# Two PSUM tiles for the transposes of batch 1, and the kv step of batch 2 after matmul 14 instead of 12

## Chip, cores and metric

The kernel runs on one core of a Trainium2 chip. Its time is the device time of one execution in microseconds, and lower is better. Before the change the median of three runs is 281.68 us (281.46 to 281.71).

## What is computed

The inputs q, k and v have the shape (batch 8, heads 8, sequence 576, head size 64). Per batch and head, q is put through a softmax over the head size, k through a softmax over the sequence; k's softmax and v make a 64×64 matrix kv, and q's softmax is multiplied by it. The result, with the heads side by side, is a matrix x of 4608 tokens by 512, which goes through two dense layers with an exact Gelu between them.

```python
q_s = exp(q - max(q, -1));  q_s = q_s / (sum(q_s, -1) + 1e-9)
k_s = exp(k - max(k, 2));   k_s = k_s / (sum(k_s, 2) + 1e-9)
kv  = einsum('bhsd,bhse->bhde', k_s, v)
x   = einsum('bhsd,bhde->bhse', q_s, kv)       # -> (4608, 512)
out = gelu(x @ w_in) @ w_out                   # 512 -> 2048 -> 512
```

## The kernel before

**Tiling.** Each batch is a block of 512 tokens; the 64 tokens left over of each of the 8 batches make a ninth block. For every block TensorE does an h phase (`h_phase`, line 300: 16 groups of four 128×512 matmuls with w_in, each group followed by a Gelu on ScalarE, line 305) and a y phase (`y_phase`, line 310: four output tiles `j`, each the sum of 16 matmuls with w_out, counted by `t`, then a copy by VectorE at line 317 and a store).

**The attention part of a batch b** is cut into small steps that are placed between those matmuls:
- `exp_q`, `exp_k` (lines 133, 138): exponentials on ScalarE, into `eq` and `ek`.
- `norm_q` (lines 196 to 198): row sums, reciprocals and the product, on VectorE and POOL; with two parts the second product is on VectorE.
- `cast_v` (line 145): v to bf16 with a column of ones, into `v_aug`, one call for each of the four head pairs.
- `kv_step`: `kv_mm` twice (line 166, 36 small matmuls each, half 0 for head pairs 0 and 1, half 1 for 2 and 3), then `kv_norm` on VectorE (lines 176, 177), which writes `kvc`.
- The transpose of q. Batches 0 and 1 do it on TensorE, in two halves of eight 128×128 transposes (`tp_mm`, line 217), each copied out of PSUM by `tp_evac` (line 226 on VectorE). Later batches use a transposing DMA (`xbar_step`, line 236).
- `x_all`, or for batch 1 single calls of `x_mm` (line 256): kv times transposed q, copied out at lines 280 and 282.

**Buffers in PSUM.** Three pools: `psum_h` with three buffers of tag "h", `psum_y` with two of tag "y", and `psum_a`, which has one buffer for each of its tags: "a", and the larger "a2". A tile of `psum_a` can be written only when the last reader of the tile before it under the same tag is done. Under "a2" come, in turn: kv of batch 0, the transposes `tp` of batch 1, kv of batch 1, two tiles of x of batch 1, kv of batch 2 and so on. Under "a" come one half of batch 0's transposes, then a tile of x of each batch.

**Order.** The order on each engine is the program's own order (`manual_schedule`): an engine works through its instructions as they are written down and waits on semaphores where another engine's result, or the release of a buffer, is needed. The transposes of batch 1 are placed in the y phase of batch 0, after twelve of the sixteen matmuls of all four output tiles:

```python
for t in range(12):
    y_part(t, range(J))
tp_step(1, 0)             # tp_mm, tp_evac of half 0
tp_step(1, 1)
cast_v(1, 3)
load(3)
cast_wo(3, wo[3], 2, 1, "s")
y_part(12, range(J))
y_part(13, range(J))
kv_step(1)
```

`cast_wo(..., "s")` (line 412) is the conversion of a quarter of the last 512 rows of w_out on ScalarE. In the y phase of batch 1, steps hang on the pair (j, t): they are issued after that matmul. The exponentials of batches 2 and 3 stand before this phase in the order exp_q(2), exp_k(2), exp_k(3), exp_q(3).

Of the kernel before, what the change touches and what calls it, by code (L numbers as in the profile page):

```python
# [9 lines left out]
BF16 = mybir.dt.bfloat16  # L10
# [6 lines left out]
def kernel(  # L17
# [20 lines left out]
    J = 4  # L38
# [16 lines left out]
    psum_a = ctx.enter_context(tc.tile_pool(name="psum_a", bufs=1, space=bass.MemoryType.PSUM))  # L55
# [25 lines left out]
    st = [dict() for _ in range(B + 1)]  # L81
# [72 lines left out]
    def kv_mm(b, half):  # L154


        if "kv" not in st[b]:
            st[b]["kv"] = psum_a.tile([128, 2, 2, 256], FP32, tag="a2", name="kv")
        ps = st[b]["kv"]
        for n in range(NS):  # L160
            for i in range(2):
                for hh in range(2):
                    hp = 2 * half + i
                    pr = slice(hh * 64, hh * 64 + 64)
                    c = slice((hh ^ i) * 64, (hh ^ i) * 64 + 64)
                    nc.tensor.matmul(  # L166
                        ps[c, i, half, 0:D + 1], ek[b % 2][pr, hp, n, :],
                        v_aug[b % 2][pr, hp, n, 0:D + 1], start=(n == 0), stop=(n == NS - 1),
                    )

    def kv_norm(b, h0, h1):

        ps = st[b]["kv"]
        m = h1 - h0
        rec = small.tile([128, 2, 2], FP32, tag="reck")
        nc.vector.reciprocal(rec[:, :, 0:m], ps[:, :, h0:h1, D])
        nc.vector.tensor_tensor(  # L177
            out=kvc[b].rearrange("p (h i) d -> p i h d", i=2)[:, :, h0:h1],
            in0=ps[:, :, h0:h1, 0:D],
            in1=rec[:, :, 0:m].unsqueeze(3).to_broadcast([128, 2, m, D]), op=ALU.mult,  # L180
        )

    def kv_step(b):
        kv_mm(b, 0)
        kv_mm(b, 1)
        kv_norm(b, 0, 2)

    def norm_q(b, i=0, n=1, eng=None):

        eng = eng or nc.gpsimd  # L190
        eq = st[b]["eq"]
        w = H // n
        hs = slice(i * w, (i + 1) * w)
        qsum = small.tile([128, J, w], FP32, tag="qsum")
        recq = small.tile([128, J, w], FP32, tag="recq")
        nc.vector.reduce_sum(out=qsum, in_=eq[:, :, hs, :], axis=AX.X)  # L196
        nc.vector.reciprocal(recq, qsum)  # L197
        eng.tensor_tensor(  # L198
            out=eq[:, :, hs, :], in0=eq[:, :, hs, :],
            in1=recq.unsqueeze(3).to_broadcast([128, J, w, D]), op=ALU.mult,  # L200
        )

    def tp_mm(b, half):
        if half == 0:
            st[b]["qT"] = attn_sb.tile([128, J, HP, 128], BF16, tag="qT", name="qT")
        if b == 1:
            if half == 0:
                st[b]["tp"] = psum_a.tile([128, 2, J, 2, 128], BF16, tag="a2", name="tp")
            ps = st[b]["tp"][:, half]
        else:  # L210
            pool, tag = (psum_h, "h") if half == 1 else (psum_a, "a")
            ps = pool.tile([128, J, 2, 128], BF16, tag=tag)
        st[b][f"tp{half}"] = ps
        for i in range(2):
            hp = 2 * half + i
            for j in range(J):
                nc.tensor.transpose(
                    ps[:, j, i, :],
                    st[b]["eq"][:, j, 2 * hp:2 * hp + 2, :].rearrange("p h d -> p (h d)"),
                    identity,  # L220
                )
# [8 lines left out]
    def tp_step(b, half):  # L230
        tp_mm(b, half)
        tp_evac(b, half)

    def xbar_step(b):
        st[b]["qT"] = attn_sb.tile([128, J, HP, 128], BF16, tag="qT", name="qT")
        nc.sync.dma_start_transpose(
            out=st[b]["qT"].rearrange("p j x m -> p (j x) m"),
            in_=st[b]["eq"].rearrange("p j h d -> p (j h d)"),
        )
# [218 lines left out]
    norm_q(0, 0, 2)  # L458
    norm_q(0, 1, 2, nc.vector)
    tp_mm(0, 0)  # L460
    tp_evac(0, 0, "s")
    table(AF.Gelu)
# [4 lines left out]
    cast_wi(0, wi[0], "p")  # L467
    cast_wi(1, wi[1], "p")
    tp_mm(0, 1)
    warm(2)  # L470
    for hp, pool, tag in ((0, psum_y, "y"), (1, psum_y, "y"), (2, psum_a, "a"), (3, psum_h, "h")):
# [38 lines left out]
    for t in range(12):  # L510
# [35 lines left out]
    y_phase(1, {  # L546
        (0, 15): [lambda: norm_q(2, 0, 2)],
        (1, 1): [lambda: norm_q(2, 1, 2, nc.vector)],
        (1, 12): [lambda: kv_step(2)],
        (1, 15): [lambda: xbar_step(2)],  # L550
        (2, 2): [lambda: cast_v_all(3), lambda: load(4)],
        (3, 5): [lambda: x_all(2), lambda: kv_step(3)],
# [65 lines left out]
```

The softmax here doesn't subtract the row's maximum and nothing guards it: scores larger than these inputs give would overflow.

## Time and profile before

| | |
|---|---|
| median of three runs | 281.68 us (281.46 to 281.71) |
| profiled execution | 281.9 us |
| its span, first to last instruction | 280.1 us |
| TensorE clock granted | 1.00 |
| TensorE busy | 271.0 us, 97% of the span |
| ScalarE busy | 157.0 us, 56% |
| VectorE busy | 102.2 us, 37% |
| POOL busy | 33.0 us, 12% |
| h matmuls (line 300) | 576, busy 126.4 us |
| y matmuls (line 310) | 560, busy 124.2 us |

Matmuls overlap in the profile: one of 128×512 shows 379 ns, while the next starts about 216 ns after it. What a step takes of TensorE's time is therefore read from start to start. The names of engines in the profile are PE (TensorE matmuls), PEld (TensorE weight loads), DVE (VectorE), ACT (ScalarE), POOL and SP; `a <- b` in brackets names what ended an idle time. Times in a timeline are counted from the first instruction of the span.

### The profile page before, as it was taken

How to read it: one execution, taken by the hardware profiler on the slowest of the kernel's cores; microseconds unless marked ns; L12 is line 12 of the kernel's file. 1: busy time of each engine (PE TensorE's matmuls, PEld its weight loads, DVE VectorE, ACT ScalarE, POOL GpSimd, SP SyncE). 2: the span in 40 equal slices, each digit the busy share in tenths (PEclk: the TensorE clock that was granted, in tenths of full speed). 3: DMA queues.
4: the chain of work that ended last, by engine and by line, in shares of the span. 5: the costliest groups of instructions: out<-in, count | busy, mean ns of one | idle time of the engine just before them, and what ended most of it. 6: DMA issues, size and time to landing. Idle time of an engine off the chain costs nothing.

```text
span 280.1 us, 4564 instructions
## 1 busy us (share of the span) xinstructions
PE 271.0 (97%) x1922; PEld 125.2 (45%) x1922; DVE 102.2 (37%) x152; ACT 157.0 (56%) x243; POOL 33.0 (12%) x25
## 2 busy tenths in 40 slices
PE   7699989999999999999999999999999999999995
PEld 3344444444544444444444444444444444444443
DVE  3767477308763530074007500552005200230012
ACT  5747664779466915692469436852683264036400
POOL 1530050002020040005000500050005000000000
PEclk9999999999999999999999999999999999999999
DMA  6999999961997129911991189126501500120033
GB/s 235 380 404 427 400 401 407 399 250 43 268 390 91 41 76 240 357 41 42 259 372 41 42 209 375 53 77 171 131 0 75 150 2 0 75 77 0 0 77 76
DMA packets 44996, 50.10 MB, mean 179 GB/s; under 512 B 20400, under 2 KB 29872, under 8 KB 44720
## 3 DMA queue, kind: packets, MB, share of 16 engines
q1 hardware_dynamic: 44688, 49.68, 53.4%
q8 instruction: 15, 0.25, 0.4%
q10 hardware_dynamic: 288, 0.13, 0.2%
q14 instruction: 5, 0.04, 0.1%
HBM read 36.70 MB, written 9.44 MB: 165 GB/s over the span
## 4 chain that ended last, share of the span: by engine, by line
PE 75%; DMA 18%; SPq 2%; ACT 2%; ACTq 0%; issue 0%; DVE 0%
PE ps L310 36%; PE ps L300 35%; DMA w<-in_moe_w_in_dram 6%; DMA f<-in_v_dram 4%; DMA w<-in_moe_w_out_dram 3%; DMA out_dram<-y_sb 3%; SPq L98 2%; DMA touch<-in_moe_w_out_dram 2%; PE kv L166 1%; PE ps L332 1%; PE ps L256 1%; ACT ek L138 1%; ACT e L133 1%; ACTq L435 0%; ACT L133 0%
## 5 line engine op out<-in xcount | busy, mean ns | idle before, releaser
L300 PE MATMUL ps<-xT,wi_bf 128*128 128x512 bf16 x576 | 126.4, 379 | 0.2
L310 PE MATMUL ps<-wo_bf,g 128*128 128x512 bf16 x560 | 124.2, 379 | 0.0
L305 ACT ACTIVATE g<-ps 128x512 bf16<-128x512 f32 x144 | 85.2, 597 | 69.3 <-PE ps L300 69.3
L300 PEld LDWEIGHTS <-wi_bf 128*128 128x128 bf16 x576 | 56.1, 98 | 69.0 <-DVE wi_bf L383 1.0
L310 PEld LDWEIGHTS <-g 128*128 128x128 bf16 x560 | 54.0, 98 | 64.6 <-issue 0.8
L317 DVE COPY y_sb<-ps 128x512 f32<-128x512 f32 x35 | 23.8, 686 | 80.9 <-PE ps L310 80.7
L198 POOL TENSOR_TENSOR e<-e,recq 128x2048 bf16<-128x2048 bf16 (+1 forms) x9 | 25.7, 2857 | 179.2 <-DVE recq L197 151.0
L145 DVE CAST v_aug<-f 128x576 bf16<-128x576 f32 x26 | 17.9, 745 | 46.4 <-DMA f<-in_v_dram 46.4
L196 DVE TENSOR_REDUCE qsum<-e 128x16 f32<-128x1024 bf16 (+1 forms) x13 | 21.0, 1614 | 15.0 <-ACT e L133 15.0
L282 ACT CAST xT<-ps 128x512 bf16<-128x512 f32 x19 | 10.2, 589 | 27.9 <-PE ps L256 18.2
L133 ACT ACTIVATE e<-f 128x512 bf16<-128x512 f32 (+1 forms) x42 | 20.5, 556 | 2.4 <-DMA f<-in_q_dram 2.1
L138 ACT ACTIVATE ek<-f 128x2304 bf16<-128x2304 f32 (+1 forms) x10 | 17.2, 1730 | 1.9 <-DMA f<-in_k_dram 1.9
L280 DVE CAST xT<-ps 128x512 bf16<-128x512 f32 x15 | 9.7, 686 | 17.7 <-PE ps L256 14.8
L79 ACT ACT_TABLE_LOAD x9 | 11.5, 1283 | 2.8 <-issue 2.6
L133 ACT ACT_TABLE_LOAD x7 | 9.0, 1283 | 0.1
L417 PE MATMUL ps<-zeros 128*128 128x512 f32 (+1 forms) x14 | 7.1, 647 | 1.5 <-DVE zeros L449 1.5
L383 DVE CAST wi_bf<-w 128x512 bf16<-128x512 f32 x12 | 7.4, 660 | 2.5 <-DMA w<-in_moe_w_in_dram 2.2
L166 PEld LDWEIGHTS <-ek 64*64 64x64 bf16 x576 | 6.3, 105 | 3.0 <-issue 1.4
L166 PE MATMUL kv<-v_aug,ek 64*64 64x65 bf16 x576 | 6.9, 193 | 0.3
L198 DVE TENSOR_TENSOR e<-e,recq 128x1024 bf16<-128x1024 bf16 x4 | 6.4, 1608 | 0.1
L256 PE MATMUL ps<-qT,kvc 64*64 64x512 bf16 x60 | 5.0, 390 | 1.0 <-DVE kvc L177 1.0
L410 DVE CAST wo_bf<-w 128x2048 bf16<-128x2048 f32 (+1 forms) x4 | 4.4, 1090 | 3.8 <-DMA w<-in_moe_w_out_dram 3.8
(35 smaller groups left out, 42.4 us busy)
## 6 DMA issues: line engine op xcount, KB each, us to landing
out_dram<-y_sb SPq DMA_DIRECT2D x32, 256.0 KB, 2.3
f<-in_k_dram SPq DMA_DIRECT2D x6, 1152.0 KB, 9.7
f<-in_v_dram SPq DMA_DIRECT2D x6, 1152.0 KB, 11.8
f<-in_q_dram SPq DMA_DIRECT2D x6, 1024.0 KB, 7.5
w<-in_moe_w_in_dram SPq DMA_DIRECT2D x6, 512.0 KB, 8.9
f<-in_k_dram SPq DMA_DIRECT2D x4, 576.0 KB, 10.1
f<-in_v_dram SPq DMA_DIRECT2D x8, 288.0 KB, 7.9
f<-in_q_dram SPq DMA_DIRECT2D x4, 512.0 KB, 12.5
```

Of the source, the lines that this page charges most:

```text
L79: nc.scalar.activation(out=scr[:, 1:2], in_=scr[:, 0:1], func=func)
L133: nc.scalar.activation(out=dst[:, i], in_=src[:, u], func=AF.Exp)
L138: nc.scalar.activation(out=ek[b % 2][:, i:i + n], in_=st[b]["kf"][:, i:i + n].rearrange("p x (n d) -> p x n d", n=NS), func=AF.Exp,)
L145: eng.tensor_copy(out=v_aug[b % 2][:, hp, :, 0:D], in_=st[b]["vf"][:, hp, :].rearrange("p (n d) -> p n d", n=NS),)
L166: nc.tensor.matmul(ps[c, i, half, 0:D + 1], ek[b % 2][pr, hp, n, :], v_aug[b % 2][pr, hp, n, 0:D + 1], start=(n == 0), stop=(n == NS - 1),)
L196: nc.vector.reduce_sum(out=qsum, in_=eq[:, :, hs, :], axis=AX.X)
L198: eng.tensor_tensor(out=eq[:, :, hs, :], in0=eq[:, :, hs, :], in1=recq.unsqueeze(3).to_broadcast([128, J, w, D]), op=ALU.mult,)
L282: nc.scalar.copy(out=st[b]["xT"][:, hp, :], in_=ps)
L300: nc.tensor.matmul(ps, wi_bf[:, dm, t * 128:(t + 1) * 128], xT[:, dm, :], start=(dm == 0), stop=(dm == NDM - 1),)
L305: nc.scalar.activation(out=g[:, t, :], in_=ps, func=AF.Gelu)
L310: nc.tensor.matmul(ps, st[c]["g"][:, t, j * 128:(j + 1) * 128], wo_bf[:, t, :], start=(t == 0), stop=(t == NDF - 1),)
L317: nc.vector.tensor_copy(out=y_sb, in_=ps)
```

## The change

Two edits. First, `tp_mm` no longer makes one "a2" tile for both halves of batch 1's transposes. Half 0 takes a tile of its own under tag "a", as half 0 of batch 0 does, and half 1 takes a tile under "a2" and uses its first part. Second, the `kv_step` of batch 2 is issued after the matmul (1, 14) of the y phase of batch 1 instead of after (1, 12).

```diff
     def tp_mm(b, half):
         if half == 0:
             st[b]["qT"] = attn_sb.tile([128, J, HP, 128], BF16, tag="qT", name="qT")
-        if b == 1:
-            if half == 0:
-                st[b]["tp"] = psum_a.tile([128, 2, J, 2, 128], BF16, tag="a2", name="tp")
-            ps = st[b]["tp"][:, half]
+        if b == 1 and half == 1:
+            ps = psum_a.tile([128, 2, J, 2, 128], BF16, tag="a2", name="tp")[:, 0]
         else:
             pool, tag = (psum_h, "h") if half == 1 else (psum_a, "a")
             ps = pool.tile([128, J, 2, 128], BF16, tag=tag)
@@
         (0, 15): [lambda: norm_q(2, 0, 2)],
         (1, 1): [lambda: norm_q(2, 1, 2, nc.vector)],
-        (1, 12): [lambda: kv_step(2)],
+        (1, 14): [lambda: kv_step(2)],
         (1, 15): [lambda: xbar_step(2)],
```

## The prediction

> **What bounds the kernel now.** I read the page's busy shares first, then the waits of TensorE, then the stretches around the two edits in order of time, engine by engine.
>
> ```profile
> PE 271.0 (97%) x1922; PEld 125.2 (45%) x1922; DVE 102.2 (37%) x152; ACT 157.0 (56%) x243; POOL 33.0 (12%) x25
> ```
>
> TensorE is busy 97% of 280.1 us and the next engine 56%. A microsecond taken off TensorE's queue therefore comes off the time, unless something else is late at the same place. So all waits of TensorE are listed:
>
> ```profile
> PE ps L217 <- POOL e L198: 2.0, 1, 2.0
> PE ps L417 <- DVE zeros L449: 1.5, 1, 1.5
> PE ps L256 <- DVE kvc L177: 1.0, 2, 0.6
> PE tp L217 <- DVE qT L226: 0.8, 1, 0.8
> ```
>
> The first three belong to the start-up. The fourth is the only one after it, and it carries the name of the tile that the change splits. In order of time, TensorE first, then VectorE:
>
> ```profile
> 39.65 0.61 PE L217 MATMUL tp<-identity,e 128*128 128x128 bf16 x8
> 41.05 0.61 PE L217 MATMUL tp<-identity,e 128*128 128x128 bf16 x8 [0.78 <-DVE qT L226]
> 41.49 1.89 PE L310 MATMUL ps<-wo_bf,g 128*128 128x512 bf16 x8
> 43.31 0.78 PE L166 MATMUL kv<-v_aug,ek 64*64 64x65 bf16 x72
> 44.02 1.25 PE L310 MATMUL ps<-wo_bf,g 128*128 128x512 bf16 x5
> ```
>
> ```profile
> 40.30 0.69 DVE L226 COPY qT<-tp 128x1024 bf16<-128x1024 bf16 x1 [0.66 <-PE tp L217]
> 41.69 0.69 DVE L226 COPY qT<-tp 128x1024 bf16<-128x1024 bf16 x1 [0.70 <-PE tp L217]
> 42.30 0.74 DVE L145 CAST v_aug<-f 128x576 bf16<-128x576 f32 x1
> ```
>
> The second eight transposes begin 0.05 us after the copy of the first eight ends at 40.99. Half 1 writes columns that the copy does not read, yet it waits for it.
>
> The second edit is at batch 2's kv. No TensorE wait is listed there, but the weight loads show one, and the chain says on whom:
>
> ```profile
> 66.92 0.67 PEld L166 LDWEIGHTS <-ek 64*64 64x64 bf16 x72 [0.62 <-ACT ek L138]
> ```
>
> ```profile
> 64.86 2.02 ACT ek L138
> 66.88 0.04 issue
> 66.92 0.78 PE kv L166 x67
> 67.70 5.50 PE ps L310 x25
> ```
>
> kv starts 0.04 us after the exponential of k(2) ends. The idle time of the weight loader overstates the stall, since it normally rests between loads; it is worked out below.
>
> **What the Trainium skill says.** *PSUM — Partial Sum Buffer*, "PSUM bank collisions raise a hardware error", forbids two engines on one bank and quadrant at once, and its "Specifications" give 2 KiB to a bank. Each half is 4·2·128 bf16 = 2,048 bytes, so the halves are in two banks before and after: the wait hangs on the shared tile, not on the bank. *TensorE: Matmul & The Clock Gate*, "Back-to-back issue gap", gives N/2.4 + 2.5 ns for isolated matmuls, 56 ns at 128 columns, and about 81 ns for streams that reload weights; here eight transposes start over 0.61 − 0.22 = 0.39 us, which is 56 ns each, so I use that. *TensorEngine Tiling (Array Packing)*, "Key Properties", says that a change of tiling mode drains TensorE; the trace agrees: eight L310 matmuls and the change to 64-row tiles take 43.31 − 41.49 = 1.82 us, where the chain's 45 matmuls in 9.71 us (0.216 each) give 1.73, so the change costs 0.09.
>
> **The change part by part.** *Half 1 in its own tile.* From the first transpose of a half to the matmul after it is 41.49 − 41.05 = 0.44 us. Half 0 starts at 39.65, so half 1 could start at 40.10 and starts at 41.05: **0.95 us** of TensorE's time goes. The trace does not show transposes following a different tile's without a wait. Bounds: 0.056 us between the two (as inside a half), or 0.31 us, the largest step at a change of shape seen above; there is none here, so I take the first, and 0.7 is the low end. A gain above 0.95 is excluded, as nothing else stands before half 1: its input is normalized by 39.03 (VectorE's 1.73 us multiply from 37.30).
>
> The buffers moved into are free: half 0 takes tag "a", last read in batch 0; half 1 takes "a2", last read by batch 0's kv. The readers that come next on them wait for copies that end before: batch 1's x on "a" comes after 44, and kv on "a2" needs only the copy of half 1.
>
> What is late next, with TensorE 0.95 earlier (kv at 42.36, its second half, where v's last quarter is first used, 0.32 later, at 42.68):
> - VectorE: the copy of half 0 stays at 40.30; half 1's follows back to back at 40.91 (at 45.31 two L317 copies of 0.68 take 1.29 together, so start 0.61 apart) and ends at 41.60; the cast of v's last quarter can then start at 41.52. Its transfer was issued at 33.1 and took 8.3, so it landed at 41.4 to 41.5: it fits within hundredths. The cast ends at 42.26, 0.4 before its use.
> - TensorE's queue: kv waits for half 1's copy (41.60), and the sequencer stood at that wait at 42.42 before, so would reach it at 41.47 and is held some 0.15 us. Three L310 matmuls lie issued ahead (0.65 us), so it costs nothing; without that cover, 0.15.
> - ScalarE's casts of the last two quarters of w_out: landings at 34.46 + 7.6 = 42.1 and 35.9 + 6.8 = 42.7, casts done at 42.74 and 43.37. Their matmuls, at 44.02 and 44.89, move to 43.07 and 43.94: 0.3 and 0.6 are left.
> - kv's normalization is done at 44.79; moved by 0.95 it stays ahead of x. From there to the kv of batch 2, no wait of TensorE is listed; the exponentials of batch 2 follow the last Gelu, which TensorE releases, so they move too. k(2) and q(2) land before 49.
>
> *kv of batch 2 two matmuls later.* By the spacing, 29 L310 matmuls from 60.38 and the 0.09 change put kv at 60.38 + 6.26 + 0.09 = 66.73; it started at 66.92: a stall of **0.19**. Two more matmuls are 0.43, so kv comes at 67.16 against a release at 66.92: the stall goes with 0.24 to spare. The step carries 72 matmuls (0.71 us), their loads, and on VectorE a reciprocal (0.17) and a product (0.42); no DMA. Between its old and new place only the two matmuls are issued, so the order on VectorE, ScalarE, POOL and SP is as before, and the q transpose by DMA still follows it. VectorE's reciprocal, which with everything behind it waits for kv, started at 68.39, behind the 1.22 us multiply from 67.25. kv's last matmul now starts 0.59 after its first, at 67.75, and 0.26 later (43.89 to 44.15 in batch 1) VectorE can act: 68.01. The multiply hides it, with 0.39 to spare. If that cover were gone, the y copy and four casts behind would shift by the 0.24, and the last cast (to 72.26) would still precede its use by kv of batch 3 at 73.59 − 0.19 by 0.9. The transposed q landed at 68.64 + 3.7 = 72.38; x needs it at 73.14 − 0.19: 0.56 left.
>
> Sum: 0.95 + 0.19 = 1.14 us. The profiled execution took 281.9 (span 280.1), 0.2 above the median of the runs; I take the gain off both: profile 280.76 with a span of 278.96, median 281.68 − 1.14 = **280.54**.
>
> **Rivals.** *Transfers take over* (0.10): v's last quarter or w_out's third lands later than in this trace. The four v transfers took 8.3 to 9.4 us, so a slip of 0.5 to 1 is conceivable; 0.4 and 0.3 are free. It costs 0.2 to 0.7: 280.7 to 281.2. Against it: the stream was issued before, at its own pace, and no engine of the change touches it. *The kv move gives nothing* (0.06): the exponential ends later against TensorE, or the stall is another; 281.68 − 0.95 = 280.73. *The wait is inherited* (0.05): half 1 is still ordered after half 0's copy, through the two-bank tag or otherwise; only 0.19 is left, 281.49, within what counts as no change. *Slower* (0.03): kv of batch 2 comes so late that its normalization holds VectorE, and with it the casts of v(3) that kv of batch 3 needs. That begins where kv is 0.24 + 0.39 + 1.14 = 1.8 us later than before (1.14 is from 72.26 to 73.40), and takes 1.14 more to cancel the gain; 4 us later would give 281.68 − 1.14 + 2.2 = 282.7. Two matmuls are a ninth of that. The forecast itself has 0.76.
>
> **How the numbers follow.** A measurement of this kernel tells about 0.2%, 0.56 us, from no change. Faster: 0.76 + 0.06 + 0.08 of the transfers' 0.10 = 0.90; within: 0.02 + 0.05 = 0.07; slower 0.03. The range runs from 280.30, below the forecast by the spread of the three runs (0.25), to 280.95, which takes in the low end of the first step (0.25 less), the rival without the kv gain, and half of the transfers'.
>
> **What would show it.** In the profile after: the wait of L217 on L226 is gone and sixteen transposes start within 0.9 us; VectorE's two L226 copies stand back to back; the cast of v starts near 41.5; kv of batch 1 starts near 42.36. Batch 2's kv follows 31 L310 matmuls, without an idle time put down to the exponential, 0.31 us after the last of them. From there on every start is 1.14 earlier. The forecast is wrong if kv of batch 1 shows a wait for v or L412 holds L310 after it, if a transpose waits on L226 or L177, or if x of batch 2 waits for the q transpose.

## The result, and the profile after

The changed kernel takes 280.44 us (280.29 to 280.69, six runs) against 281.69 (281.43 to 282.0, six runs): a ratio of 0.9956, 95% interval 0.9943 to 0.9969, a gain of 1.25 us. Measured again further below, it is 280.42 against 281.59. The forecast was 280.54 in 280.30 to 280.95. The profiled span went from 280.1 to 278.9 us.

The busy shares of the page after, and all waits of TensorE after (columns: who waited for whom, total us, times, longest). Its line numbers are smaller by two than those of before, for all that stands after the first edit: L215 are the transposes, L308 the y matmuls, L298 the h matmuls, L254 x.

```profile
PE 272.2 (98%) x1922; PEld 125.8 (45%) x1922; DVE 102.1 (37%) x152; ACT 157.0 (56%) x243; POOL 33.0 (12%) x25
```

```profile
PE ps L415 <- DVE zeros L447: 1.5, 1, 1.5
PE ps L254 <- DVE kvc L177: 1.0, 2, 0.6
PE ps L215 <- POOL e L198: 0.4, 1, 0.4
```

Only the waits of the start-up are left. The one of the transposes on the copy, 0.8 us before, is gone. It was a wait that the program carried: before, the first transpose of half 1 waits on VectorE's semaphore, and in the changed kernel it carries no wait for VectorE. The timeline at the transposes, TensorE and then VectorE (start, duration, what):

```profile
39.52 0.61 PE L215 MATMUL ps<-identity,e 128*128 128x128 bf16 x8
39.97 0.61 PE L215 MATMUL tp<-identity,e 128*128 128x128 bf16 x8
40.42 1.89 PE L308 MATMUL ps<-wo_bf,g 128*128 128x512 bf16 x8
42.24 0.78 PE L166 MATMUL kv<-v_aug,ek 64*64 64x65 bf16 x72
42.95 1.47 PE L308 MATMUL ps<-wo_bf,g 128*128 128x512 bf16 x6
```

```profile
40.17 0.69 DVE L224 COPY qT<-ps 128x1024 bf16<-128x1024 bf16 x1 [0.65 <-PE ps L215]
40.78 0.68 DVE L224 COPY qT<-tp 128x1024 bf16<-128x1024 bf16 x1
41.38 0.75 DVE L145 CAST v_aug<-f 128x576 bf16<-128x576 f32 x1
```

Half 1 follows half 0 after 0.45 us, where it was 41.05 − 39.65 = 1.40: 0.95 us. The copies stand back to back, 0.61 apart, and v's cast behind them. That cast is held by two things at once: v's last quarter, issued at 33.00, landed at 41.36, 0.02 before it. The casts of the last two quarters of w_out's last 512 rows, on ScalarE:

```profile
42.02 1.25 ACT L410 CAST wo_bf<-w 128x512 bf16<-128x512 f32 x2 [2.12 <-DMA w<-in_moe_w_out_dram]
```

The first of the two (0.62 us) ends at 42.64, and the y matmul that needs it, the one behind kv, starts at 42.95: 0.31 later. The timeline of TensorE at kv of batch 2, and the only wait of the weight loader there:

```profile
59.30 6.85 PE L308 MATMUL ps<-wo_bf,g 128*128 128x512 bf16 x31
66.09 0.78 PE L166 MATMUL kv<-v_aug,ek 64*64 64x65 bf16 x72
66.80 5.14 PE L308 MATMUL ps<-wo_bf,g 128*128 128x512 bf16 x23
71.86 0.63 PE L254 MATMUL ps<-qT,kvc 64*64 64x512 bf16 x8
```

```profile
PEld L166 <- ACT ek L138: 0.4, 1, 0.4
```

kv starts 66.09 − 59.30 = 6.79 us after the first of 31 matmuls, which at 0.216 each take 6.70: the 0.09 of the change of tiling mode and nothing else. The weight loader still shows a wait that is put down to the exponential, 0.4 where it was 0.6. That is not a stall: the loader rests 0.42 before x of batch 2 as well, where the profile names nobody. Only the 0.2 above that was lost time. The exponential itself ended at 65.80, 0.29 before kv; where kv waits for it, kv starts 0.05 after it ends.

The chain that ended last, over the stretch of both edits (start, us, what). Before, it left TensorE at kv of batch 2 for the exponential. Now TensorE hands over to itself from 22.89 on:

```profile
22.89 6.43 PE ps L298 x29
29.33 10.36 PE ps L308 x48
39.69 0.45 PE ps L215 x8
40.13 0.45 PE tp L215 x8
...
59.47 6.69 PE ps L308 x31
66.16 0.71 PE kv L166 x68
```

From the first transpose of batch 1 to x of batch 2 TensorE took 73.14 − 39.65 = 33.48 us before and 71.86 − 39.52 = 32.34 after: **1.14 us**, the sum of the prediction. Another 0.13 lies ahead of the transposes, in the start-up, which neither edit touches, and 0.06 is lost behind x (207.04 us from x to the end of the span instead of 206.98), which makes the 1.21 of the span.

### The profile page after: what moved, and what is told of

It reads as the page before. It is cut to its first block, busy times and chain, and to the rows that moved or that the text cites. A ratio compares the mean times of both kernels' runs of the same rounds, so it can differ in the third digit from the quotient of the medians.

```text
span 278.9 us, 4564 instructions
## 1 busy us (share of the span) xinstructions
PE 272.2 (98%) x1922; PEld 125.8 (45%) x1922; DVE 102.1 (37%) x152; ACT 157.0 (56%) x243; POOL 33.0 (12%) x25
## 4 chain that ended last, share of the span: by engine, by line
PE 91%; DMA 7%; DVE 1%; ACTq 0%; issue 0%
PE ps L308 44%; PE ps L298 42%; DMA w<-in_moe_w_in_dram 3%; DMA f<-in_v_dram 2%; PE kv L166 2%; DMA touch<-in_moe_w_in_dram 2%; PE ps L254 1%; PE ps L330 1%; DVE wi_bf L381 0%; ACTq L433 0%; PE ps L259 0%; PE ps L215 0%; PE tp L215 0%; DVE y_sb L335 0%; PE xx L254 0%
## 5 line engine op out<-in xcount | busy, mean ns | idle before, releaser
L298 PE MATMUL ps<-xT,wi_bf 128*128 128x512 bf16 x576 | 126.4, 379 | 0.3
L308 PE MATMUL ps<-wo_bf,g 128*128 128x512 bf16 x560 | 124.2, 379 | 0.0
L298 PEld LDWEIGHTS <-wi_bf 128*128 128x128 bf16 x576 | 56.2, 98 | 68.9 <-DVE wi_bf L381 1.0
L308 PEld LDWEIGHTS <-g 128*128 128x128 bf16 x560 | 53.9, 98 | 64.6 <-issue 0.8
L415 PE MATMUL ps<-zeros 128*128 128x512 f32 (+1 forms) x14 | 8.6, 764 | 1.5 <-DVE zeros L447 1.5
L254 PE MATMUL ps<-qT,kvc 64*64 64x512 bf16 x60 | 5.0, 390 | 1.0 <-DVE kvc L177 1.0
```

The costliest lines, as they stand in the source:

```text
L298: nc.tensor.matmul(ps, wi_bf[:, dm, t * 128:(t + 1) * 128], xT[:, dm, :], start=(dm == 0), stop=(dm == NDM - 1),)
L308: nc.tensor.matmul(ps, st[c]["g"][:, t, j * 128:(j + 1) * 128], wo_bf[:, t, :], start=(t == 0), stop=(t == NDF - 1),)
```

## The experiments

All are read in the same way. "Begin" is the start of the first transpose of batch 1; "half" is from there to that of half 1; "kv(2)" is from the matmul before kv of batch 2 to kv; "to x" is from the begin to x of batch 2. Ratios are to the kernel before, measured together with it (its median was 281.69 for the first row of the changed kernel, 281.57 for the four rows from "tiles only" to "shared tile, slow copy", 281.59 for the others). Several of these differences in time are inside each other's intervals; the steps of the traces tell them apart.

| kernel | begin | half | kv(2) | to x | median | ratio (95%) |
|---|---|---|---|---|---|---|
| before | 39.65 | 1.39 | 0.51 | 33.48 | | |
| changed | 39.52 | 0.45 | 0.31 | 32.34 | 280.44 | 0.9956 (0.9943 to 0.9969) |
| tiles only | 39.74 | 0.45 | 0.51 | 32.54 | 280.74 | 0.9969 (0.9958 to 0.9980) |
| kv only | 39.58 | 1.39 | 0.31 | 33.29 | 281.39 | 0.9993 (0.9983 to 1.0003) |
| shared tile, copies last | 39.07 | 0.45 | 0.51 | 32.66 | 280.60 | 0.9963 (0.9950 to 0.9976) |
| shared tile, slow copy | 39.05 | 1.71 | 0.51 | 33.80 | 281.83 | 1.0013 (1.0002 to 1.0024) |
| v's cast late | 39.45 | 0.45 | 0.31 | 33.16 | 281.18 | 0.9982 (0.9973 to 0.9991) |
| kv after (1, 10) | 39.56 | 0.45 | 0.94 | 32.97 | 281.00 | 0.9981 (0.9974 to 0.9988) |
| kv after (1, 13) | 38.97 | 0.45 | 0.31 | 32.47 | 280.39 | 0.9961 (0.9946 to 0.9976) |
| changed, again | 39.28 | 0.45 | 0.31 | 32.34 | 280.42 | 0.9955 (0.9940 to 0.9969) |
| v's quarter last | 40.19 | 0.45 | 0.31 | 33.23 | 281.42 | 0.9996 (0.9982 to 1.0011) |

**The tiles alone.** The diff against the changed kernel:

```diff
-        (1, 14): [lambda: kv_step(2)],
+        (1, 12): [lambda: kv_step(2)],
```

> The two tiles alone, kv of batch 2 where it was, after matmul (1, 12). Theory (two waits, which add): half 1's transposes follow half 0's 0.056 us apart, 0.95 us of TensorE's time goes, and kv of batch 2 still starts 0.04 us after the exponential of k(2), 0.51 us after the matmul before it. Time 281.69 - 0.95 = 280.74. Rival (the kv stall depends on where the transposes leave TensorE, so the first edit shortens it too): kv of batch 2 starts 0.31 us after the matmul before it, and the time is that of the changed kernel, 280.5. Rival (part of the gain of 1.25 is not of the edits): half 1 gains 0.95 or less and the time stays above 280.9.

From its timeline of TensorE:

```profile
39.74 0.61 PE L215 MATMUL ps<-identity,e 128*128 128x128 bf16 x8
40.19 0.61 PE L215 MATMUL tp<-identity,e 128*128 128x128 bf16 x8
59.52 6.42 PE L308 MATMUL ps<-wo_bf,g 128*128 128x512 bf16 x29
66.07 0.78 PE L166 MATMUL kv<-v_aug,ek 64*64 64x65 bf16 x72
```

It went as the theory has it: 33.48 − 32.54 = 0.94 us "to x", and kv of batch 2 keeps its step of 0.51. The time is 0.83 below that of before. The second wait does not shrink with the first, because the exponential moves with TensorE: in all eleven profiled executions it ends 6.50 us after the first y matmul of batch 1.

**kv alone.** The diff against the kernel before:

```diff
-        (1, 12): [lambda: kv_step(2)],
+        (1, 14): [lambda: kv_step(2)],
```

> kv of batch 2 after matmul (1, 14) alone, the transposes in their shared tile. Theory: kv starts 0.31 us after the matmul before it, where it was 0.51, and its first matmul 0.2 us after the exponential's end; half 1's transposes still wait 0.78 us for the copy of half 0. Gain 0.2 us: 281.5, hardly to be told from no change by the time; the starts in the trace decide. Rival: the stall moves with kv (it is not the exponential that it waits for), 0.51 us again, 281.7.

From its timeline of TensorE:

```profile
40.98 0.61 PE L217 MATMUL tp<-identity,e 128*128 128x128 bf16 x8 [0.78 <-DVE qT L226]
67.09 0.78 PE L166 MATMUL kv<-v_aug,ek 64*64 64x65 bf16 x72
```

The wait of the transposes is there, that of kv is not: 0.20 us "to x". By the time alone, 0.18 with an interval over 1, it could not have been told. The two edits add: 0.94 + 0.20 = 1.14.

**One tile, copies after both halves.** The diff against the kernel before:

```diff
-    tp_step(1, 0)
-    tp_step(1, 1)
+    tp_mm(1, 0)
+    tp_mm(1, 1)
+    tp_evac(1, 0)
+    tp_evac(1, 1)
```

> The kernel before, with its one tile for both halves, and both copies issued after both halves of transposes; kv of batch 2 stays at (1, 12). Theory (half 1 waits only because it stands after the copy of half 0 on the same tile): the sixteen transposes run without a wait, 0.95 us goes as with two tiles. If the copy of half 0 waits for all sixteen, the copies start at about 40.75 on VectorE instead of 40.30, the cast of v's last quarter ends 0.45 later, at 42.7, and kv's second half waits for it by less than 0.1. Time 280.7 to 280.85. Rival (half 1 waits for something else of the one tile, its buffer or its bank): a wait of TensorE in the transposes remains, 281.5 or more.

The timeline of TensorE, and of VectorE:

```profile
39.07 1.06 PE L217 MATMUL tp<-identity,e 128*128 128x128 bf16 x16
```

```profile
40.17 1.29 DVE L226 COPY qT<-tp 128x1024 bf16<-128x1024 bf16 x2 [0.92 <-PE tp L217]
41.37 0.74 DVE L145 CAST v_aug<-f 128x576 bf16<-128x576 f32 x1
```

With one tile and the same two banks the sixteen transposes run without a wait: what held half 1 was its place behind the copy on a shared tile. The first copy starts 40.17 − 39.07 = 1.10 us after the first transpose, where it is 0.65 with two tiles; so it waits for all sixteen. Two tiles let VectorE start on half 0 at once.

What that is worth the run does not show. kv takes 0.85 us to the next matmul instead of 0.71, so 0.14 is lost, but the wait that ends last there is another one. From the timelines of TensorE and ScalarE:

```profile
41.79 0.86 PE L166 MATMUL kv<-v_aug,ek 64*64 64x65 bf16 x72
42.63 1.46 PE L310 MATMUL ps<-wo_bf,g 128*128 128x512 bf16 x6
```

```profile
41.97 1.25 ACT L412 CAST wo_bf<-w 128x512 bf16<-128x512 f32 x2 [2.97 <-DMA w<-in_moe_w_out_dram]
```

kv's second half waits some 0.06 us for v's cast, as expected ("less than 0.1"). The y matmul behind kv needs the first of ScalarE's two casts of the last rows of w_out (their third quarter), which ends at 42.58, and it starts 0.05 after that. This execution began its transposes 0.45 earlier than the changed kernel's, but w_out's quarter came only 0.05 earlier (41.97 against 42.02). By these numbers two tiles would have lost as much here. The time, 280.60, is not told apart from the 280.74 of the tiles alone. One tile with the copies last and kv after (1, 14) was not run.

**One tile, a slower copy.** The diff against the kernel before:

```diff
-    tp_step(1, 0)
+    tp_mm(1, 0)
+    tp_evac(1, 0, "s")
```

> The kernel before, with half 0 copied by ScalarE instead of VectorE, which took 0.99 us for such a copy in batch 0 against 0.69; ScalarE is idle there from 39.99 to 42.12. Theory (the stall is the copy's length and two signals): half 1's transposes start 0.3 us later than before, 1.25 us of stall against 0.95, and the time rises by 0.3 to 282.0. VectorE has one copy less, so its cast of v is not later. Rival (the stall hangs on VectorE's queue or on a fixed cost of changing halves): half 1 starts as before or earlier, 281.7 or less.

TensorE's and ScalarE's timelines:

```profile
40.76 0.61 PE L217 MATMUL tp<-identity,e 128*128 128x128 bf16 x8 [1.10 <-ACT qT L228]
```

```profile
39.70 1.01 ACT L228 COPY qT<-tp 128x1024 bf16<-128x1024 bf16 x1 [0.54 <-PE tp L217]
```

The copy is 0.32 longer (1.01 against 0.69) and half 1 starts 0.32 later (1.71 against 1.39): the stall is the copy's length plus the signals. The time rises by 0.26 (interval 0.06 to 0.68).

**v's cast late.** The diff against the changed kernel:

```diff
     tp_step(1, 1)
+    nc.vector.memset(zeros32, 0.0)
+    nc.vector.memset(zeros32, 0.0)
     cast_v(1, 3)
```

> The changed kernel with two fills of 128x512 fp32 by VectorE (0.49 us each at the start of the kernel, 0.97 together; what they write is not read afterwards) between the copies of the transposes and the cast of v's last quarter. Theory (that cast has 0.4 us to spare before kv of batch 1 uses it, and nothing after it on VectorE has less): kv's second half starts 0.97 - 0.38 = 0.6 us late, and the time is 280.44 + 0.6 = 281.0. Rival (no cover, the chain copy, cast, kv is what sets the time after the change): 0.97 us late, 281.4. Rival (kv does not hang on this cast): no change, 280.4.

VectorE's and TensorE's timelines:

```profile
41.44 0.48 DVE L512 MEMSET zeros<- 128x512 f32 x1
42.09 0.48 DVE L513 MEMSET zeros<- 128x512 f32 x1 [0.17 <-DVE zeros L512]
42.50 0.69 DVE L145 CAST v_aug<-f 128x576 bf16<-128x576 f32 x1
```

```profile
43.24 0.47 PE L166 MATMUL kv<-v_aug,ek 64*64 64x65 bf16 x34 [0.58 <-DVE v_aug L145]
```

The second fill waited for the first, which the expectation had not counted. Against half 1's first transpose the cast ends 43.19 − 39.89 = 3.30 us later, where in the changed kernel it is 42.13 − 39.97 = 2.16: 1.14 of delay. kv to the next matmul takes 1.49 instead of 0.71, so 0.78 comes through, and the cover is 1.14 − 0.78 = 0.36 us, near the 0.4 of the prediction. The time is 0.7 above the changed kernel's.

**kv of batch 2 after (1, 10) and after (1, 13).** The diffs against the changed kernel replace `(1, 14)` by `(1, 10)` and by `(1, 13)`.

> The changed kernel with kv of batch 2 after matmul (1, 10), four matmuls earlier than in the change and two earlier than before it. Theory (the start is set by the end of the exponential of k(2), whatever stands before it): TensorE stands still for 0.20 + 2 x 0.216 = 0.63 us before kv, and the time is 280.44 + 0.63 = 281.07. Rival (the loss of 0.2 was a cost of that place and not a wait for the exponential): 0.2 us or less, 280.65.

> The changed kernel with kv of batch 2 after matmul (1, 13), one earlier. Theory: one matmul is 0.216 us, the wait that it replaces was 0.20, so kv comes 0.02 us after the release and waits at most a few hundredths; time as with the change, 280.4. Rival (a release has to stand 0.1 us or more before its use to cost nothing, since the weights are loaded ahead): kv starts 0.4 us after the matmul before it instead of 0.31.

TensorE's timeline after (1, 10):

```profile
65.89 0.78 PE L166 MATMUL kv<-v_aug,ek 64*64 64x65 bf16 x72 [0.56 <-ACT ek L138]
```

The step before kv is 0.94, so 0.63 of stall, as worked out: each matmul taken away from in front of kv puts its 0.216 back as waiting. After (1, 13) the step is 0.31, not the 0.4 of its rival. One matmul would have done, and by the steps (0.216 − 0.20) a release some 0.02 us ahead is enough: kv starts 0.07 after the exponential's end, where it starts 0.05 after it when it waits.

That kernel's execution also met the rival of the transfers. The timelines of VectorE, TensorE and ScalarE after (1, 13):

```profile
41.25 0.75 DVE L145 CAST v_aug<-f 128x576 bf16<-128x576 f32 x1 [0.34 <-DMA f<-in_v_dram]
```

```profile
41.68 0.85 PE L166 MATMUL kv<-v_aug,ek 64*64 64x65 bf16 x72
42.54 0.81 PE L308 MATMUL ps<-wo_bf,g 128*128 128x512 bf16 x3
```

```profile
41.87 1.24 ACT L410 CAST wo_bf<-w 128x512 bf16<-128x512 f32 x2 [2.58 <-DMA w<-in_moe_w_out_dram]
```

In this execution the transposes began at 38.97. VectorE stood idle for v's last quarter, and kv took 42.54 − 41.68 = 0.86 instead of 0.71: 0.15 of a head start of 0.55 was lost. v cost kv's second half some 0.05, but what set the loss was again w_out: the first of the two casts ended at 42.49, and the y matmul behind kv, which waits for it, started 0.05 later. With v in time it would have started no earlier. No run moved this cast alone: this is read from the trace, not shown by an experiment.

After (1, 10) v's quarter was late without any loss. From VectorE's timeline:

```profile
40.82 0.68 DVE L224 COPY qT<-tp 128x1024 bf16<-128x1024 bf16 x1
41.63 0.75 DVE L145 CAST v_aug<-f 128x576 bf16<-128x576 f32 x1
```

The transposes began at 39.56, as in the changed kernel, but the quarter landed at 41.60 instead of 41.36, and the cast stands 0.81 behind the copy instead of 0.60. kv of batch 1 still took 0.71: the cover held.

**The change again, and v's last quarter fetched last.** The second kernel issues the last quarter of v of batch 1 after the two last quarters of w_out. `load_pair` gets a fifth argument, which it calls ahead of its last part; that part of the edit is left out here:

```diff
-    load_pair(1, "v", v, 4)
-    load_wo_end(wo[3])
+    load_pair(1, "v", v, 4, lambda: load_wo_end(wo[3]))
```

> The changed kernel once more, for more runs against the kernel before. Theory (the two edits bring 0.95 + 0.20 and the start-up varies by itself between executions): the median lies 1.15 below that of before, 280.4 to 280.5, and the trace shows again 0.45 us from the first transpose of half 0 to that of half 1 and 0.31 before kv of batch 2, wherever the transposes begin (they began at 38.97 to 39.74 so far). Rival (the change also shortens the start-up): the transposes begin before 39.5 and the gain is above 1.3.

> The changed kernel with the last quarter of v of batch 1 fetched after the two last quarters of w_out instead of before them (512 KB, which landed over 1.3 us). Theory (the transfer is what is late next after the change, with 0.4 us free in an execution whose transposes begin near 39.5): the quarter lands 1.3 later, at 42.6, its cast ends at 43.4 and kv's second half waits about 0.85 us for it; the time is 281.3. Where the transposes begin at 39.0 the wait is 1.4 and hides that head start. Rival (v's transfer has much more room than 0.4): the time stays at 280.4 to 280.6.

The change again brings 1.17 us, with the same steps as at first: 32.34 "to x". Its transposes began at 39.28, without the gain above 1.3 that a shorter start-up was to bring. From VectorE's and TensorE's timelines with v's quarter last:

```profile
43.29 0.75 DVE L147 CAST v_aug<-f 128x576 bf16<-128x576 f32 x1 [1.17 <-DMA f<-in_v_dram]
```

```profile
44.10 0.48 PE L168 MATMUL kv<-v_aug,ek 64*64 64x65 bf16 x34 [0.69 <-DVE v_aug L147]
```

kv to the next matmul takes 44.51 − 42.90 = 1.61 us: 0.90 lost, against 0.85 expected, and the time is 1.0 above the changed kernel's measured beside it, nearly the whole gain. Two absolute times of the expectation were missed by some 0.66 each, which cancels: the quarter landed at 43.27 instead of 42.6, and the transposes began at 40.19 instead of 39.5, as the whole start-up ran later. Counted from the begin, it landed 3.08 us on, where it is 1.83 in the changed kernel: 1.25 later, near the 1.3.

So v's transfer can take the gain when it slips by 1.3. It is not the nearest limit: in the changed kernel v has 0.36 us to spare, and the third quarter of w_out's last 512 rows has less, as worked out below. No experiment pointed to a kernel faster than the change.

## Why the prediction was right

- **The first edit, 0.95.** Measured 0.95. The choice of 0.056 us between the halves, against a low end with 0.31, was right: the sixteen starts are evenly spaced across the border of the two tiles.
- **What is late next.** Corrected for the begin (0.13 earlier), kv of batch 1 was forecast at 42.23 and came at 42.24; v's cast at 41.39 and came at 41.38. The sequencer's wait for half 1's copy cost nothing, as its cover said: kv follows the matmul before it by the 0.31 of any change of mode. The cover of v's cast, 0.4, measured 0.36. That of w_out's third quarter, 0.3, was the smaller of the two, and measured 0.31; a matmul that waits for such a cast starts 0.05 after its end (after (1, 13)), so 0.26 of it is free.
- **The second edit, 0.19.** Measured 0.20. VectorE's reciprocal started at 67.33, behind the multiply that runs from 66.18 to 67.41, so moving kv cost nothing there.
- **The sum.** 1.14 forecast, 1.14 between transposes and x. The medians give 1.25 and 1.17, and the interval of the first, 0.87 to 1.61 us, is wider than their distance from 1.14. Some luck is in the agreement to the hundredth: the profiled execution of the change began its transposes at 39.52. The one after (1, 13), which began at 38.97, has the same two steps and gained 33.48 − 32.47 = 1.01.
- **The rivals.** "The wait is inherited" and "the kv move gives nothing" are excluded by the halves of the change run alone. "Transfers take over" is real at a small size: 0.14 and 0.15, where the prediction had 0.2 to 0.7. It named the right two transfers, but had them landing late against a fixed begin. That slip was seen after (1, 10), 0.25 us, and was covered. Where something was lost (copies last, and after (1, 13)), TensorE had arrived 0.45 and 0.55 us early, and by the traces w_out's quarter set the loss. "Slower" was not seen.

## What to carry to other kernels

A tile that two engines use in halves can order the halves as one, as here: where the producer's second half stood behind the consumer's first, the producer stalled for the consumer's whole instruction. Separate tiles, or issuing both productions first, removed this; separate tiles also left the consumer its early start (0.65 us after the first transpose instead of 1.10), though no run shows a gain in time from that. Size a stall from start to start against the normal step, not from an idle time that the profile puts down to somebody, and list what comes late next, with its margin, before counting the gain as whole. Where two waits stand one behind the other, as v's cast and w_out's did, the one that ends last sets the loss.

## What the runs showed of the hardware

The begin of batch 1's transposes moved between 38.97 and 40.19 us over the eleven profiled executions, though no edit stands ahead of it except the new order of three DMAs in the last. Part of it is the arrival of w_in: the last eight of VectorE's L383 casts ran from 20.56 in the kernel before, and two h matmuls at 22.50 and 23.02 came 0.42 and 0.52 us after the one before instead of 0.22; with the copies last the casts ran from 19.59, and there were no such steps. The four executions without such steps there began their transposes at 38.97 to 39.28, the seven with one or both at 39.44 to 40.19. The spread, 0.77 us without the last kernel and 1.22 with it, is near the first edit's gain, so in single executions only the steps inside a trace can be compared.
